# Causal attention with memory and two MoE blocks: scores of the last 64 queries for two pairs of heads at once, four rounds per couple of pairs

## The chip, the core and the metric

One core of a Trainium2 chip. The time is device microseconds (us) of one execution of the whole program, as the median of several runs. The engines of a core run side by side, each in its own order of instructions: PE (TensorE: matmuls and transposes), DVE (VectorE), ACT (ScalarE), POOL (GpSimd); SP only issues transfers. PEld is PE's loading of weights.

## The reference

```python
def _attn_ref(q, k, v, M_prev, z_prev, beta):          # B, H, S, D = 4, 8, 576, 64
    scores = scale * np.matmul(q, k.transpose(0, 1, 3, 2))
    causal = np.triu(np.ones((S, S), dtype=bool), k=1)
    scores = np.where(causal, -1000000000.0, scores)
    scores = scores - scores.max(-1, keepdims=True)
    a = np.exp(scores)
    a /= a.sum(-1, keepdims=True) + 1e-09
    local = np.matmul(a, v)
    ...
    mem_out = mem_ret / mem_norm                        # phi(q) @ M_prev, over phi(q) @ z_prev
    g = 1.0 / (1.0 + np.exp(-beta))[None, :, None, None]
    return g * mem_out + (1 - g) * local

def _moe_ref(x, w1, w2, w3, w_out):                     # 2304 tokens, 512 -> 1024 -> 512
    return ((x @ w1) * (x @ w2) @ w3) @ w_out

def _moe2_ref(x, w_in, w_out):                          # 512 -> 2048 -> 512
    h = x @ w_in
    return (h - np.tanh(h)) @ w_out
```

## The kernel before

The program has three stages: attention (to about 232 us), the first block of three products (to about 560), the second block (to the end). Only the attention is touched. Every instruction goes through one helper, so the profile gives all of them line 50; they are told apart by the names of their tiles.

**Attention.** The 32 heads (4 batches of 8) lie in 16 *pairs* `P`: head `h` of a pair has the 64 rows 64h to 64h+63 of the tile `r` (q and k, transposed, float32). The 576 queries of a head are five groups `u`: u = 0 to 3 with 128 queries, u = 4 with the last 64. A group needs keys 0 to 128(u+1) only, the last one all 576.

- `scores(m)`: a float32 matmul of 64 rows (the head's 64 dimensions) by 64 columns (64 queries) takes one quarter of PE's array. For u = 0 to 3 the two heads are the two row halves, the two halves of the 128 queries the two column halves (loop variable `y`), so that four matmuls use four quarters. For u = 4 there are only 64 queries: head h uses the quarter (rows h, columns h), two quarters at a time, and the 576 keys go in two parts of 288. Small bfloat16 matmuls (`maskb`) add the causal mask. Results lie in `sc`, a tile of two PSUM banks; there are two such tiles (`SB = 2`).
- `rmax(m)`: DVE takes the negated row maxima from `sc` into `st`. `exps(m)`: ACT writes exp(sc - max) to `p` and the sums to `st`; then that `sc` tile is free. `recip(m)` on DVE and `norm(m)` on POOL divide `p` by the sums, one round later.
- `trans(P, u)`: PE transposes `p` in blocks of 128 into `t` (two PSUM banks); ACT and DVE copy them to `g` (`g0` for u = 0, 1, `g1` for u = 2, 3 and the last group, `g2` for that group's last 64 keys). `av(P, grp)`: PE multiplies `g` by `v` into `o`, ACT copies that to `xs`. `av(P, 0)` is the queries of u = 0, 1 and `av(P, 1)` the rest.

**The order** of all engines within the attention is the order of the source (a helper chains each instruction to the one before it on its engine). A step `m` is one entry of `GROUPS = ((0, 1), (2,), (3,), (4,))`, so a pair has four steps, and the loop takes two steps at a time, a *round*: even rounds hold u = 0, 1 and u = 2, odd rounds u = 3 and u = 4. One round is, in this order: `recip` and `norm` of the two steps before; `scores` and `rmax` of both steps; `work(m)` (the exps of the first step and background jobs); one `av` of the pair before; `pieces` (see below); `trans` of the round before's first step; `work(m + 1)`; `pieces`; `trans` of its second step.

**Background.** `decode` jobs turn 30 loaded blocks of weights (`raw`, 512 KB each) into two float32r halves by operations on POOL (`T`, `E`, and the copy to `zs`, `fo`, `wa` or `wb`), ACT (`T`, `E`) and DVE; a new one begins at every step up to `LEAD`, then at every second. `fold_pe` multiplies w3 by w_out in pieces of three matmuls (`fo`), up to `PIECES[s]` of them at each of a pair's four steps. The memory part (`mw`, `mq`, `mt`, `mo`) runs as a job, too. After the last round the matmuls of the first block (`ab`) follow; PE may take them while it would wait in the last rounds.

**First loads.** SP's queue issues two parts of pair 0's `r`, three `raw`, then `r` of pair 1; ACT's queue issues the identity, the mask, the third part of pair 0's `r`, and `beta` (`gates`).

Of the kernel before, what the change touches and what calls it, by code (L numbers as in the profile page):

```python
# [33 lines left out]
def block_kernel(ctx, tc, qk, qt, vt, mp, zp_d, beta, w1, w2, w3t, wo, wi, wo2, ident_d, mask_d, out):  # L34
# [138 lines left out]
    def tp(o, i):  # L173
# [7 lines left out]
    PIECES = (1, 2, 0, 2)  # L181
    MEM, ROOM = 12, (1.5, 1.5, 1.75)
    LEAD, SHORT, TB, WX = 3, 9, 4, (0, 1, 2, 3, 4, 5)
# [9 lines left out]
        ("r", RB), ("1", 1), ("2", 2), ("4", 4), ("z", ZB), ("t", TB))]  # L193
# [58 lines left out]
    jobs, todo, raws, live = [], deque(fold_seq), [], [0]  # L252
# [7 lines left out]
    def decode(item):  # L260
# [4 lines left out]
        t = apt.tile([128, 512], U32, tag="T", name="T")  # L265
# [3 lines left out]
        e = ap2.tile([128, 512], U32, tag="E", name="E")  # L269
# [22 lines left out]
        DV.tensor_tensor(out=lo, in0=tf, in1=hi.bitcast(F32), op=ALU.subtract)  # L292
        if k[0] in range(8):
            folds.append((k, fstep[0]))
# [37 lines left out]
    if True:  # L332
# [6 lines left out]
        qk_cols(0, slice(320, 576), AC)  # L339
# [12 lines left out]
        first_q(320, 576)  # L352
# [38 lines left out]
        GROUPS = ((0, 1), (2,), (3,), (4,))  # L391
        NM = 16 * len(GROUPS)
# [3 lines left out]
        def step(m):  # L396
            P, s = divmod(m, len(GROUPS))
            return P, [(u, 128 * x) for x, u in enumerate(GROUPS[s])]

        def scores(m):  # L400
            P, us = step(m)
            q, k = qk_t[P][:, 0], qk_t[P][:, 1]
            hr = [(h, slice(64 * h, 64 * h + 64)) for h in range(2)]
            sc = sc_t[m] = pss.tile([128, 2, 512], F32, tag="sc", name="sc")
            qs = [(h, r, y, slice(64 * y, 64 * y + 64)) for y in range(2) for h, r in hr]
            for u, a in us:
                if u == 4:
                    continue
# [24 lines left out]
        def exps(m):  # L433
            P, us = step(m)
            st = st_t[m]
            for x, (u, a) in enumerate(us):
                sc = seen(m, u, a)
                p = p_t[P, u] = ap3.tile([128, PW[u]], F32, tag=f"p{u}", name="p")
                p = p[:].rearrange("p (a n) -> p a n", a=2)
# [34 lines left out]
        def trans(P, u):  # L474
            p = p_t.pop((P, u))
            if u == 0:
                g_t[0] = ap2.tile([128, 2, 2, 256], F32, tag="g0", name="g0")
            if u == 2:
                g_t[1] = ap1.tile([128, 4, 2, 320], F32, tag="g1", name="g1")
                g_t[2] = ap1.tile([64, 2, 64], F32, tag="g2", name="g2")  # L480
            if u < 4:
                K = 128 * u + 128
                blocks = [(kb, h) for kb in range(u + 1) for h in range(2)]
                for c in range(0, len(blocks), 4):
# [4 lines left out]
                    G = g_t[0] if u < 2 else g_t[1]  # L489
# [3 lines left out]
            else:  # L493
                t = psT.tile([128, 4, 128], F32, tag="t", name="t")
# [10 lines left out]
        def av(P, grp):  # L505
# [4 lines left out]
            hr = [(h, slice(64 * h, 64 * h + 64)) for h in range(2)]  # L510
# [4 lines left out]
            else:  # L515
                for kb in range(4):
                    q0 = 128 if kb == 3 else 0
                    for h, r in hr:
                        mm(o[r, q0:320], v[:, kb, h], g_t[1][:, kb, h, q0:320], kb == 0, False)
                for h, r in hr:  # L520
                    mm(o[r, 256:320], v[0:64, 4, h], g_t[2][:, h], False, True)
# [186 lines left out]
        coming, begun, active, owed = [0], [0], [0], [0]  # L708
        ahead()

        def background(m):
# [13 lines left out]
            if m >= coming[0] and begun[0] < len(fold_seq) and active[0] < TB:  # L725
# [15 lines left out]
        load_qk(1)  # L741
# [27 lines left out]

        m = 0  # L770
        while m < NM + 3 or jobs or late or folded[0] < 16 or begun[0] < len(fold_seq):
            P, s = divmod(m, 4)
# [6 lines left out]
            if m < NM:  # L779
                fill(FILL["s"].get(m, 0))  # L780
                for h in (m, m + 1):
                    scores(h)
                    rmax(h)
                if m == 0:
                    set_gates()
                if m == 2:
                    first_q(0, 576, 1)
            work(m)
            if 1 <= P <= 16:
                av(P - 1, s // 2)  # L790
                if s == 2 and P + 1 < 16:
                    load_v(P + 1)
            trs = 0 <= m - WAIT < NM
            flush_t()
            pieces(m, PIECES[s])
            if trs:
                fill(FILL["t"].get(m, 0))
                for u in GROUPS[(m - WAIT) % 4]:
                    trans((m - WAIT) // 4, u)
# [4 lines left out]
            if trs:  # L804
                for u in GROUPS[(m + 1 - WAIT) % 4]:
                    trans((m + 1 - WAIT) // 4, u)
# [383 lines left out]
```

## Time and profile before

| | |
|---|---|
| three runs | 968.78 us median (968.11 to 969.84) |
| the profiled execution | 971.45 us, its span 969.7 us |
| PE busy | 943.9 us, 97% of the span |
| DVE, ACT, POOL busy | 675.8, 623.1, 408.1 us (70, 64, 42%) |
| granted TensorE clock | 0.996 of full (2.4 GHz) on average |

The profiled execution took 971.45 us; its first to last instruction is the span, and 1.75 us lie around it. It is 2.67 us (0.28%) above the median of the runs. In the views, a row of the timeline or of the chain has its start and its duration; "x8" is the number of instructions merged into it (a float32 matmul of scores has two records); in square brackets stands idle time of the engine before the row and what ended it.

### The profile page before, as it was taken

What the parts mean: (1) busy time and instruction counts of PE and PEld (TensorE: products, weight loads), DVE (VectorE), ACT (ScalarE), POOL (GpSimd) and SP (SyncE); (2) the same over time, 40 slices, a digit from 0 to 9 for tenths busy, and PEclk for the clock granted to TensorE, in tenths of its full rate; (3) what the DMA queues carried; (4) which work ended last, traced back from release to release, by engine and by line L of the source; (5) the groups of instructions that cost most, each with busy time, mean ns of one, the idle gap of its engine ahead of it and who ended that gap; (6) DMA issues with size and microseconds to landing.
All of it is one profiled execution on the core that took longest, in us unless ns stands there. A gap on an engine that the chain in (4) does not pass through costs nothing.

```text
span 969.7 us, 16290 instructions
## 1 busy us (share of the span) xinstructions
PE 943.9 (97%) x5928; PEld 816.4 (84%) x5928; DVE 675.8 (70%) x1185; ACT 623.1 (64%) x1398; POOL 408.1 (42%) x500
## 2 busy tenths in 40 slices
PE   6899999999999999999999999999999999999998
PEld 3466666567989999999999999999999989999996
DVE  5778868897776743534424588887787887878875
ACT  5688887786546551323625587687777766776864
POOL 3768867786474521202406862222222222222222
PEclk9899999999999999999999999999999999999999
DMA  6455435422344530101401100000000000000000
GB/s 216 155 169 168 158 127 183 135 75 85 128 149 146 183 114 31 55 22 44 153 22 45 44 1 1 1 33 1 1 33 1 33 1 1 33 1 1 33 1 33
DMA packets 26080, 68.29 MB, mean 70 GB/s; under 512 B 4880, under 2 KB 5904, under 8 KB 26000
## 3 DMA queue, kind: packets, MB, share of 16 engines
q1 hardware_dynamic: 25296, 66.86, 20.8%
q8 instruction: 46, 0.75, 0.3%
q10 hardware_dynamic: 704, 0.40, 0.2%
q14 instruction: 34, 0.28, 0.1%
HBM read 62.53 MB, written 4.72 MB: 69 GB/s over the span
## 4 chain that ended last, share of the span: by engine, by line
PE 84%; DVE 7%; ACT 4%; POOL 2%; issue 1%; DMA 1%; ACTq 0%; DVEq 0%; POOLq 0%; SPq 0%
PE o L50 24%; PE h L50 21%; PE ab L50 19%; PE x L50 10%; PE sc L50 3%; PE t L50 3%; PE fo L50 3%; DVE st L50 2%; ACT p L50 2%; PE mo L50 2%; POOL p L50 1%; DMA r<-in_qk 1%; DVE g L50 1%; DVE mst L50 1%; DVE T L50 1%
## 5 line engine op out<-in xcount | busy, mean ns | idle before, releaser
L50 POOL TENSOR_TENSOR gl<-s,gh 128x384 fp32r<-128x384 f32 x96 | 99.7, 1038 | 288.0 <-ACT gh L50 274.9
L50 PE MATMUL x<-abh,wf 128*128 128x384 f32 x384 | 107.0, 342 | 1.1 <-ACT abh L50 1.1
L50 ACT ACTIVATE s<-u,pc 128x384 f32<-128x384 f32 x192 | 107.7, 613 | 0.6 <-POOL gl L50 0.6
L50 PE MATMUL ab<-xh,wa 128*128 128x384 f32 x384 | 106.9, 338 | 0.7 <-ACT xh L50 0.6
L50 POOL TENSOR_SCALAR p<-p,st 128x128 f32<-128x128 f32 (+2 forms) x144 | 86.1, 616 | 47.2 <-DVE st L50 41.0
L50 PE MATMUL ab<-xh,wb 128*128 128x384 f32 x384 | 105.9, 336 | 0.0
L50 DVE SCALAR_TENSOR_TENSOR s<-s,u 128x384 f32<-128x384 f32 x96 | 83.9, 874 | 26.8 <-ACT s L50 25.9
L50 ACT ACTIVATE p<-sc,st 128x128 f32<-128x128 f32 (+2 forms) x144 | 78.3, 556 | 29.7 <-DVE st L50 25.8
L50 ACT ACTIVATE u<-u,pc 128x384 f32<-128x384 f32 x96 | 59.4, 619 | 46.8 <-DVE s L50 46.8
L50 DVE TENSOR_TENSOR a<-ab,a 128x384 f32<-128x384 f32 x48 | 26.4, 552 | 77.4 <-PE ab L50 77.4
L50 PEld LDWEIGHTS x<-abh,wf 128*128 128x128 f32 x384 | 70.2, 188 | 5.6 <-issue 3.9
L50 POOL TENSOR_SCALAR E<-raw 128x512 f32<-128x512 f32 x72 | 53.9, 749 | 48.5 <-DVE z2p L50 13.1
L50 DVE TENSOR_TENSOR t<-h,t 128x384 f32<-128x384 f32 x96 | 53.1, 553 | 28.0 <-ACT t L50 27.5
L50 PEld LDWEIGHTS ab<-xh,wa 128*128 128x128 f32 x384 | 70.1, 188 | 2.0 <-ACT xh L50 0.9
L50 ACT ACTIVATE u<-h 128x384 f32<-128x384 f32 x96 | 46.7, 487 | 38.9 <-PE h L50 38.8
L50 PEld LDWEIGHTS ab<-xh,wb 128*128 128x128 f32 x384 | 70.1, 188 | 0.3 <-issue 0.3
L50 POOL TENSOR_SCALAR T<-raw 128x512 f32<-128x512 f32 x72 | 53.7, 746 | 39.2 <-DMA raw<-in_wo 12.0
L50 PE MATMUL sc<-r 64*64 64x128 f32 (+4 forms) x640 | 64.5, 457 | 5.8 <-DMA r<-in_qk 2.9
L50 DVE SCALAR_TENSOR_TENSOR s<-s,s 128x384 f32<-128x384 f32 x96 | 63.9, 665 | 8.7 <-DVE s L50 0.5
L50 PE MATMUL t<-ident,p 128*128 128x128 f32 (+1 forms) x400 | 58.2, 279 | 11.9 <-POOL p L50 4.4
L50 PEld LDWEIGHTS t<-ident,p 128*128 128x128 f32 (+1 forms) x400 | 45.2, 140 | 24.4 <-POOL p L50 6.4
L50 ACT ACTIVATE E<-raw 128x512 uint16<-128x512 uint32 x72 | 57.2, 795 | 12.6 <-POOL E L50 12.3
(208 smaller groups left out, 2538.3 us busy)
## 6 DMA issues: line engine op xcount, KB each, us to landing
raw<-in_wo SPq DMA_DIRECT2D x24, 512.0 KB, 3.5
r<-in_qk SPq DMA_DIRECT2D x15, 576.0 KB, 5.9
raw<-in_w3t SPq DMA_DIRECT2D x16, 512.0 KB, 4.0
raw<-in_w SPq DMA_DIRECT2D x16, 512.0 KB, 3.7
raw<-in_wi SPq DMA_DIRECT2D x16, 512.0 KB, 3.5
v<-in_vt SPq DMA_DIRECT2D x16, 320.0 KB, 2.9
mw<-in_qt SPq DMA_DIRECT2D x18, 256.0 KB, 3.5
out<-ob SPq DMA_DIRECT2D x18, 256.0 KB, 2.2
```

What stands on the lines that cost most here:

```text
L50: i = call(*args, **kw)
```

## The change

Two consecutive pairs, 2b and 2b + 1, now make a couple. `SEQ` gives the couple's eight steps, in four rounds:

| round | steps | `av` in it | transposes in it |
|---|---|---|---|
| s = 0 | first pair u = 0, 1; u = 2 | none | last groups of the couple before, the second head first |
| s = 2 | first pair u = 3; second pair u = 0, 1 | couple before, first pair, grp 1 | first pair u = 0, 1; u = 2 |
| s = 4 | second pair u = 2; u = 3 | couple before, second pair, grp 1; this couple, first pair, grp 0 | first pair u = 3; second pair u = 0, 1 |
| s = 6 | both last groups | second pair, grp 0 | second pair u = 2; u = 3 |

The last groups of both pairs are scored in one go, `scores_last`: one `sc` tile per head, rows of PE by head, columns by pair, so that four quarters work; both `sc` tiles are written from the start. The `p` of the second head's last groups takes the tile `p2`. The transposed last groups are copied in two halves, one per pair, one on ACT and one on DVE (twice: 128 partitions by 4x64, and 64 by 64). `g0` has one buffer in place of two, `g1` one for each pair of the couple. The buffers `T` and `E` of the decodes are now partly those that the later stages own, and a decode begins only when the fourth before it is done. `r` of two pairs is loaded in round s = 6 and scaled on ACT one and three rounds later. `r` of pair 0 comes in three parts through SP's queue, `r` of pair 1 right behind it and ahead of the `raw`; the scaling of the third part and of pair 1 moves behind the first maxima on DVE. `LEAD` is 2 in place of 3, and the loop runs one round longer at its end.

```diff
-    PIECES = (1, 2, 0, 2)
+    PIECES = (1, 2, 0, 2, 0, 2, 1, 2)
-    LEAD, SHORT, TB, WX = 3, 9, 4, (0, 1, 2, 3, 4, 5)
+    LEAD, SHORT, TB, WX = 2, 9, 4, (0, 1, 2, 3, 4, 5)
...
-        qk_cols(0, slice(320, 576), AC)
+        qk_cols(0, slice(320, 576))
...
-        first_q(320, 576)
...
-        GROUPS = ((0, 1), (2,), (3,), (4,))
-        NM = 16 * len(GROUPS)
+        SEQ = ((0, (0, 1)), (0, (2,)), (0, (3,)), (1, (0, 1)), (1, (2,)), (1, (3,)), (0, (4,)), (1, (4,)))
+        NM = 64
...
-            if us[0][0] == 4:
-                for x in range(2):
+
+        def scores_last(m):
+            P, us = step(m)
+            sc = [pss.tile([128, 2, 512], F32, tag="sc", name="sc") for _ in hr]
+            sc_t[m], sc_t[m + 1] = sc
+            for y in range(2):
+                for j, c in hr:
+                    q, k = qk_t[P + j][:, 0], qk_t[P + j][:, 1]
                     for h, r in hr:
-                        y = x ^ h
-                        mm(sc[r, y, 0:288], q[r, 512:576], k[r, 288 * y:288 * y + 288], True, y == 0)
+                        mm(sc[h][c, y, 0:288], q[r, 512:576], k[r, 288 * y:288 * y + 288], True, y == 0)
+            for j, c in hr:
                 for h, r in hr:
-                    mm(sc[r, 1, 224:288], identb[r, r], maskb[r, 0:64], False, True)
+                    mm(sc[h][c, 1, 224:288], identb[r, r], maskb[r, 0:64], False, True)
...
-                copy(g_t[1][:].rearrange("p a b q -> p (a b) q")[:, :, 256:320],
-                     t[:].rearrange("p a (b q) -> p (a b) q", b=2))
+                for j in range(2):
+                    copy(g_t[1, j][:, :, h, 256:320], t[:, :, 64 * j:64 * j + 64], on_act=j == 0)
                 t = psT.tile([128, 4, 128], F32, tag="t", name="t")
                 tp(t[0:64, 0], p[:, 512:576])
-                copy(g_t[2][:], t[0:64, 0].rearrange("p (b q) -> p b q", b=2), on_act=False)
+                for j in range(2):
+                    copy(g_t[1, j][0:64, 3, h, 0:64], t[0:64, 0, 64 * j:64 * j + 64], on_act=j == 0)
...
+        load_qk(1)
         ahead()
...
-            if m >= coming[0] and begun[0] < len(fold_seq) and active[0] < TB:
+            if m >= coming[0] and begun[0] < len(fold_seq) and active[0] < TB and turn[0] - 4 not in going:
...
-        load_qk(1)
...
+                if s == 6:
+                    scores_last(m)
                 for h in (m, m + 1):
-                    scores(h)
+                    if h == 1:
+                        first_q(320, 576)
+                    if h == 3:
+                        first_q(0, 576, 1)
+                    if s < 6:
+                        scores(h)
                     rmax(h)
...
-            if 1 <= P <= 16:
-                av(P - 1, s // 2)
...
+            if s == 2 and 1 <= b <= 8:
+                av(2 * b - 2, 1)
...
+            if s == 4 and 1 <= b <= 8:
+                av(2 * b - 1, 1)
...
+            if s in (4, 6) and b < 8:
+                av(2 * b + (s == 6), 0)
+            lots = (m - 2, m - 1) if s else (m - 1, m - 2)
...
-            if s == 0 and 1 <= P <= 16 - RB:
-                load_qk(P + RB - 1)
-            if s == 0 and 1 <= P < 15:
-                scale_q(P + 1)
+            if s == 6:
+                for P in (2 * b + 3, 2 * b + 4):
+                    if P < 16:
+                        load_qk(P)
+            if s == 0 and 1 <= b < 8:
+                scale_q(2 * b + 1)
+            if s == 4 and b < 7:
+                scale_q(2 * b + 2)
```

Two places show what stands where now. First PE, in the steady part of the attention: of a round that begins with u = 0, 1 and u = 2, what follows the scores, up to the next round's first scores. Before (`o` is `av`, `fo` the fold's pieces, `t` the transposes of the round before's two steps, u = 3 and then u = 4):

```order
L50 MATMUL o<-g_810,v_108 64x256 x2
L50 MATMUL o<-g_810,v_108 64x128 x2
L50 MATMUL fo<-wa_375,zs 128x512 x3
L50 MATMUL t<-ident,p 128x128 x8
L50 MATMUL fo<-wb_429,zs 128x512 x3
L50 MATMUL t<-ident,p 128x128 x4
L50 MATMUL t<-ident,p 64x128
L50 MATMUL sc<-r 64x512 x4
```

And now:

```order
L50 MATMUL fo<-wa_290,zs 128x512 x3
L50 MATMUL t<-ident,p 128x128 x4
L50 MATMUL t<-ident,p 64x128
L50 MATMUL fo<-wb_346,zs 128x512 x3
L50 MATMUL fo<-wa_377,zs 128x512 x3
L50 MATMUL t<-ident,p 128x128 x4
L50 MATMUL t<-ident,p 64x128
L50 MATMUL sc<-r 64x512 x4
```

The `av` has left this round, and the first transposes are those of a last group, whose `p` was the last thing that ACT wrote in the round before. In the rounds of steps 8, 48 and 56 the order has less `fo` there: none in the first two, one piece ahead of the transposes and none after in the third.

Second ACT, in the round that ends just ahead of the last groups' scores: from the exps of its first step to those of its second. Before (a round of u = 3 and u = 4; the exps of u = 4 free the second `sc` tile):

```order
L50 ACTIVATE p,st<-sc,st 128x512 x2
L50 ACTIVATE xs_354<-o,omgt 128x2x64
L50 ACTIVATE xs_445<-o,omgt 128x3x64
L50 ACTIVATE g_1004<-t 128x2x128
L50 ACTIVATE T<-T 128x512
L50 ACTIVATE p,st<-sc,st 128x576
```

And now, in round s = 4 (its second step is u = 3):

```order
L50 ACTIVATE p,st<-sc,st 128x384 x2
L50 ACTIVATE xs_607<-o,omgt 128x5x64
L50 ACTIVATE xs_1886<-o,omgt 128x4x64
L50 ACTIVATE g_1812<-t 128x4x128
L50 ACTIVATE E<-raw 128x512
L50 ACTIVATE p,st<-sc,st 128x512 x2
L50 ACTIVATE g_1912<-t 128x2x128
```

The exps that free the second `sc` tile now stand behind the copies of two `av` (5 and 4 times 64 columns) and of a whole chunk of transposes.

## Rows read from the trace of the kernel before

**Rows 1.** Stretches: us, busy time by engine, PEclk, DMA share, GB/s

```profile
25.00:35.00 10.00, 8.38 (x45) 4.26 (x47) 6.60 (x12) 6.23 (x15) 7.00 (x13) 0.66 0.46 165
...
64.88:147.50 82.62, 80.14 (x756) 52.58 (x760) 66.51 (x140) 69.48 (x188) 64.39 (x93) 1.00 0.47 158
147.50:232.00 84.50, 80.94 (x762) 52.74 (x763) 75.25 (x157) 64.64 (x177) 63.63 (x88) 1.00 0.38 130
...
300.00:560.00 260.00, 260.00 (x1539) 253.44 (x1538) 121.81 (x209) 113.69 (x228) 93.51 (x101) 1.00 0.24 76
```

**Rows 2.** The chain in two full rounds, 51.98 to 64.88 us: start, duration, what

```profile
51.98 1.60 PE sc L50 x26
53.58 0.81 PE o L50 x8
54.39 0.90 PE fo L50 x3
55.30 0.87 PE t L50 x8
56.17 0.70 PE fo L50 x3
56.87 0.71 PE t L50 x5
57.59 2.08 PE sc L50 x19
59.66 2.35 PE o L50 x20
62.02 0.81 PE t L50 x6
62.82 1.39 PE fo L50 x6
64.21 0.67 PE t L50 x6
```

**Rows 3.** Timeline of PE, 111.2 to 113.5 us: scores of u = 3 and u = 4

```profile
111.30 1.09 PE L50 MATMUL sc<-r 64*64 64x512 f32 x8
...
112.25 1.16 PE L50 MATMUL sc<-r 64*64 64x288 f32 x8
...
113.37 0.49 PE L50 MATMUL o<-g,v 128*64 128x320 f32 x2
```

**Rows 4.** Groups by form, 57 to 232 us: count, busy, mean ns, idle before

```profile
L50 POOL TENSOR_SCALAR p<-p,st 128x576 f32<-128x576 f32 x12 | 9.0, 747 | 0.0
...
L50 DVE COPY g<-t 128x512 f32<-128x512 f32 x25 | 17.2, 688 | 15.3 <-PE t L50 15.2
...
L50 DVE COPY g<-t 128x256 f32<-128x256 f32 x12 | 5.0, 419 | 3.6 <-PE t L50 3.5
...
L50 DVE COPY g<-t 64x128 f32<-64x128 f32 x13 | 3.6, 276 | 1.9 <-PE t L50 1.9
...
L50 ACT ACTIVATE g<-t 128x512 f32<-128x512 f32 x37 | 22.8, 616 | 6.6 <-PE t L50 6.5
L50 ACT ACTIVATE E<-raw 128x512 uint16<-128x512 uint32 x23 | 18.5, 804 | 0.0
L50 ACT ACTIVATE p<-sc,st 128x512 f32<-128x512 f32 x26 | 17.7, 693 | 7.7 <-DVE st L50 7.7
```

**Rows 5.** Timeline of all engines, 0 to 58 us: waits of the first rounds

```profile
10.76 1.87 PE L50 MATMUL sc<-r 64*64 64x384 f32 x8 [2.86 <-DMA r<-in_qk]
...
23.07 0.64 POOL L50 TENSOR_SCALAR T<-raw 128x512 f32<-128x512 f32 x1 [1.52 <-DMA raw<-in_wo]
...
25.40 0.33 PE L50 MATMUL t<-ident,p 128*128 128x128 f32 x1 [2.67 <-POOL p L50]
...
52.98 2.08 POOL L50 TENSOR_SCALAR p<-p,st 128x512 f32<-128x512 f32 x3 [2.73 <-DVE st L50]
```

**Rows 6.** Issues of transfers: queue, count, KB each, median us to landing

```profile
r<-in_qk SPq DMA_DIRECT2D x15, 576.0 KB, 5.9
```

More of the change, by code (lines that the diff above doesn't have):

```diff
@@ L251, in block_kernel @@
     folds, fstep, folded, fold_open = deque(), [0], [0], [False]
-    jobs, todo, raws, live = [], deque(fold_seq), [], [0]
+    jobs, todo, raws, live, turn, going = [], deque(fold_seq), [], [0], [0], set()
     def ahead():
@@ L264, in decode @@
         lw, hw = rb[:, :, 0], rb[:, :, 1].bitcast(F32)
-        t = apt.tile([128, 512], U32, tag="T", name="T")
+        n = turn[0]
+        turn[0] += 1
+        going.add(n)
+        t = (stg["T"] if n & 2 else apt).tile([128, 512], U32, tag="T", name="T")
         tf = t[:].bitcast(F32)
@@ L268, in decode @@
         yield 0, 0, 0.7
-        e = ap2.tile([128, 512], U32, tag="E", name="E")
+        e = (stg["E"] if n & 1 else ap1).tile([128, 512], U32, tag="E", name="E")
         PO.tensor_scalar(out=e[:].bitcast(F32), in0=hw, scalar1=2.0 ** -100, scalar2=2.0 ** -53,
@@ L396, in step @@
         def step(m):
-            P, s = divmod(m, len(GROUPS))
-            return P, [(u, 128 * x) for x, u in enumerate(GROUPS[s])]
+            b, s = divmod(m, 8)
+            j, us = SEQ[s]
+            return 2 * b + j, [(u, 128 * x) for x, u in enumerate(us)]
+        hr = [(h, slice(64 * h, 64 * h + 64)) for h in range(2)]
         def scores(m):
@@ L402, in scores @@
             q, k = qk_t[P][:, 0], qk_t[P][:, 1]
-            hr = [(h, slice(64 * h, 64 * h + 64)) for h in range(2)]
             sc = sc_t[m] = pss.tile([128, 2, 512], F32, tag="sc", name="sc")
@@ L437, in exps @@
                 sc = seen(m, u, a)
-                p = p_t[P, u] = ap3.tile([128, PW[u]], F32, tag=f"p{u}", name="p")
-                p = p[:].rearrange("p (a n) -> p a n", a=2)
+                p = p_t[P, u] = ap3.tile([128, PW[u]], F32, tag="p2" if u == 4 and P % 2 else f"p{u}", name="p")
+                p = p[:, 0:576 if u == 4 else PW[u]].rearrange("p (a n) -> p a n", a=2)
                 for h in [slice(0, 1), slice(1, 2)] if u < 4 else [slice(0, 2)]:
@@ L476, in trans @@
             if u == 0:
-                g_t[0] = ap2.tile([128, 2, 2, 256], F32, tag="g0", name="g0")
+                g_t[0] = ap1.tile([128, 2, 2, 256], F32, tag="g0", name="g0")
             if u == 2:
-                g_t[1] = ap1.tile([128, 4, 2, 320], F32, tag="g1", name="g1")
-                g_t[2] = ap1.tile([64, 2, 64], F32, tag="g2", name="g2")
+                g_t[1, P % 2] = ap1.tile([128, 4, 2, 320], F32, tag=f"g1{P % 2}", name="g1")
             if u < 4:
@@ L509, in av @@
             o = psA.tile([128, 512], F32, tag="o", name="o")
-            hr = [(h, slice(64 * h, 64 * h + 64)) for h in range(2)]
             if grp == 0:
@@ L768, in work, with lot @@
                 background(h)
+        def lot(h):
+            P, us = step(h)
+            for u, _ in us:
+                trans(P, u)
         m = 0
-        while m < NM + 3 or jobs or late or folded[0] < 16 or begun[0] < len(fold_seq):
-            P, s = divmod(m, 4)
+        while m < NM + 5 or jobs or late or folded[0] < 16 or begun[0] < len(fold_seq):
+            b, s = divmod(m, 8)
             fstep[0] = m
@@ L785, in block_kernel @@
                     set_gates()
-                if m == 2:
-                    first_q(0, 576, 1)
             work(m)
-            if 1 <= P <= 16:
-                av(P - 1, s // 2)
-                if s == 2 and P + 1 < 16:
-                    load_v(P + 1)
-            trs = 0 <= m - WAIT < NM
-            flush_t()
+            flush_t()
+            if s == 2 and 1 <= b <= 8:
+                av(2 * b - 2, 1)
+                if b < 8:
+                    load_v(2 * b)
+            if s == 4 and 1 <= b <= 8:
+                av(2 * b - 1, 1)
+                if b < 8:
+                    load_v(2 * b + 1)
+            if s in (4, 6) and b < 8:
+                av(2 * b + (s == 6), 0)
+            lots = (m - 2, m - 1) if s else (m - 1, m - 2)
+            trs = 0 < m <= NM
             pieces(m, PIECES[s])
@@ L797, in block_kernel @@
                 fill(FILL["t"].get(m, 0))
-                for u in GROUPS[(m - WAIT) % 4]:
-                    trans((m - WAIT) // 4, u)
+                lot(lots[0])
             work(m + 1)
@@ L804, in block_kernel @@
             if trs:
[L805 to L806 removed]
+                lot(lots[1])
             if sums and not fold_open[0]:
                 flush_o()
[L809 to L812 removed]
+            if s == 6:
[6 more added lines that the diff above has]
+                scale_q(2 * b + 2)
             if not todo and not raws and not wdec[0]:
```

12 lines of the change are left out of this document (6 added, 6 removed).

## The prediction, made before the changed kernel ran

> **What bounds the kernel now.** I read the busy time by stretches first [rows 1]. From 300 to 560 us PE is busy without a gap, so what the attention gains or loses ahead of that is passed on whole; the order behind the attention's last rounds is the same in both programs. In the attention PE has a gap of 2.5 us in 64.9 to 147.5 and of 3.6 us in 147.5 to 232: it is the bound, but not by far. In the first stretch ACT is busy 84% and DVE 80%, in the second DVE 89%. Then I read the chain through two full rounds [rows 2]: PE alone, 5.61 us (51.98 to 57.59) and 7.29 (to 64.88), 12.90 per pair and 25.8 per couple. So less PE work makes a round shorter only as long as what PE waits for in it (POOL's p, ACT's exps, copies by ACT and DVE) is ready earlier too, and none of them has much room. Before 58 us it is different: PE waits for loads and for POOL [rows 5], and from 25 to 35 us the granted clock was 0.66 of full, in part at the lower of the two levels (1.2 GHz), after the stretch in which PE stood 2.67 us.
>
> **Term 1, the scores of the last groups.** The timeline shows both kinds side by side [rows 3]. u = 3 runs on four quarters: 8 records, 4 matmuls of 512 columns, and from its start to that of the next scores 0.95 us (111.30 to 112.25), masks included. u = 4 on two quarters: also 8 records, of 288 columns only, and 1.12 us (112.25 to 113.37). At four quarters the 512 columns cost 0.95 us for 128 queries; at two, 2 x 288 = 576 columns in turn cost about as much for 64. `scores_last` puts 16 records into the same number of turns, two per quarter, so that a couple pays 1.12 us once where it paid it twice. The masks, four in place of twice two, go beside each other as those of u = 3 do. Eight couples: 8 x 1.12 = 9.0 us less of PE. Below: 0 if the quarters do not run side by side. Matmuls, transposes and `av` are otherwise the same in number.
>
> **Term 2, the transposes of the last groups come first in round s = 0.** From the chain's pieces [rows 2] the round's PE work is now scores 1.60, a piece 0.90, five transposes 0.71, two pieces 1.39, five transposes 0.71: 5.3 us, of which only 1.60 + 0.90 = 2.5 lie ahead of the first transposes, where 1.60 + 0.81 + 0.90 = 3.3 did. What they need: the last exps, then on DVE the copies of the previous transposes and two reciprocals, then on POOL the two `norm` of 0.75 us each [rows 4], the needed one second. In the round of rows 2 POOL began its norms 1.0 us after the first scores, after waiting for DVE [rows 5]; now DVE's copy ahead of it is of four blocks, not two, which is 0.27 us more (0.69 to 0.42) [rows 4]. So p is ready about 1.3 + 1.5 = 2.8 us into the round: a wait of 0.3 to 0.5 us where a piece stands ahead, and 1.2 in the rounds of steps 8 and 48, where none does. Step 56 has one piece ahead and none between, so it goes with the former. Five times 0.4 and twice 1.2: 4.4 us; I take 4.0, as DVE's copy is at times done sooner. Bounds 0 (ACT ends its last exps early, as the round s = 6 has the fewest) and 10 (1.2 or more in all seven).
>
> **Term 3, both score tiles at once.** `scores_last` needs both `sc` tiles free at the start of round s = 6; the second tile was wanted about 0.95 us into a round before. What frees it are the exps of u = 3 on ACT, which stand behind the copies of two `av`. On PE the round s = 4 is about 1.8 for the scores (u = 2 and u = 3; 0.95 the latter), 2.35 + 0.81 for the `av`, 0.87 for eight transposes, 1.39 for pieces, 0.67 for six [rows 2]: 7.9 us. On ACT: 1.8 + 3.16 + half of 0.87, then a chunk's copy of 0.62, E 0.80, and two exps of 0.69 [rows 4]: 8.2 us. Overlap of ACT's instructions takes some of that off, so 0.25 us of wait per couple: 2.0 us. Bounds 0 and 0.5 each (4.0).
>
> **Term 4, more copies.** A pair's last group cost DVE one copy of 0.28 us (64x128) and ACT one of 0.62. Now each has 128x256 and 64x64. On DVE that is 0.42 [rows 4] and about half to all of 0.28, so 0.35 more per pair; ACT loses about as much as it gains. Where DVE has room this is nothing; in 147.5 to 232 us, six pairs, it is 2.1 us on an engine that is busy 89% [rows 1]: I count half, 1.0 us, bounds 0 and 2.1.
>
> **Term 5, the start.** The third part of pair 0's `r` made PE wait 2.86 us and land at 10.76 [rows 5]. Now it follows the second part in one queue, ahead of the three `raw` and not beside them; I expect the scores of u = 2 at about 8 to 9. But half of it comes back: pair 1's u = 0, 1 are now scored in the second round, and their q is scaled on DVE behind the maxima of u = 3, while PE waits up to 2 us. The `raw` move behind another 576 KB; POOL's first `T` was not late by them. The fourth `raw` held POOL at 23.07, its norms behind it and PE for 2.67 us [rows 5]; with `LEAD` 2 that `T` stands behind the norms of two more steps, which covers it. Against it the first round with last groups has its waits for both tiles and for `g0`. Then the clock: 10 us at 0.66 cost 3.4 us [rows 1]; the new order has weak stretches there as well, so I count half of it. Together I take 3.0 us less, bounds 1 more and 6 less.
>
> **Costed at nothing.** `r` of the odd pairs is loaded one round ahead of its scaling, not two: the load needs only the scores of round s = 6 to be over and has then the rest of that round and most of the next, about 11 us, for a transfer of 5.9 us [rows 6]. If it were late, ACT would stand at the scaling with the exps of two steps behind it. One buffer of `g0`: the `av` that reads it stands ahead of the transposes that write it. Round s = 6 asks for `g0` after 1.1 us of scores, which cover a copy of 0.7. The rule that a decode begins only after the fourth before it is done shifts pieces to the end, five of them, where PE has the products of the first block beside them.
>
> **Sum.** -9.0 + 4.0 + 2.0 + 1.0 - 3.0 = -5.0 us on 971.45: 966.45 for such an execution. The runs' median is 2.67 below the profiled one, so 963.8 us.
>
> **The rivals.**
> - *All covers hold.* If terms 2 to 4 are nothing, as PE's gap of 6 us in 167 [rows 1] would have it, -12 us: 956.8.
> - *The evacuation becomes the bound.* ACT's and DVE's work per couple does not shrink, and a round's length is then their chain (maxima, exps, copies, reciprocals), not PE's sum. For it speaks DVE's 89%; against it that PE had two rounds without a gap [rows 2]. Term 1 is then waited away but for 1 us or so, and the start's 3 us half: about 966 to 969, no measurable change; 968. The Trainium skill, "TensorEngine Tiling (Array Packing)", Performance Considerations, "PSUM Bottleneck", says that tiling speeds up TensorE but not the emptying of PSUM, which may become the limit. By that rule the gain of term 1 would go, and the time is this rival's; the trace's 97% of PE against 80 to 89% of DVE bears it out only in the last third.
> - *Slower, by ACT in round s = 4.* Term 3 with the odd work that ACT has in some rounds (a partial sum's copy, the memory's exp, `mq`): three more instructions of about 0.6 us each [rows 4] put the exps 1.9 us behind PE in every couple, 15 us in all. With the other terms -9.0 + 4.0 + 15.2 + 1.0 - 3.0 = +8: 977; with six of the eight couples hit (11.4 us) it is 973, which I take. It decides where the wait passes 0.9 us per couple.
> - *The quarters do not run side by side.* In u = 3 the two matmuls of one row half read the same keys; now they read the tiles of two pairs. No row of before shows that. Then term 1 is 0, PE's longer scores cover term 3, and the time is 971.45 + 4.0 + 1.0 - 3.0, less 2.67: 970.8. Nothing in the trace speaks for it, since the matmuls are separate instructions there too.
>
> **How the numbers follow.** Chances: the forecast 0.46 (its own range 960 to 967), all covers 0.20, evacuation 0.14, slower by ACT 0.14, no quarters 0.06. A measurement of this kernel can tell about 0.2%, 1.9 us: faster is under 966.8, slower over 970.7. Faster: 0.43 of the forecast and 0.20 of the covers, with 0.02 of the evacuation: 0.65. Same: 0.03 of the forecast, 0.11 of the evacuation, 0.03 of the two last: 0.17. Slower: 0.18. The range goes from the full gain, 956.5, to where the slower cases begin, 971.
>
> **What would show it.** PE's `sc` of 64x288: 16 records within some 1.1 us, 8 couples, its total down by half. Waits "PE t <- POOL p" about 0.4 us in rounds s = 0, and "PE sc <- ACT p" about 0.25 us ahead of the last groups. DVE's busy share over 90% from 147 us on. The scores of u = 2 at 8 to 9 us, and no wait of POOL for a `raw` near 23 us. I am wrong if round s = 4 or s = 6 shows PE waiting over 1 us in most couples, or if PE's gaps in the steady part grow past 9 us.

## The result and the profile after

The changed kernel is slower by 0.9%: 977.82 us (median, 975.75 to 979.43) against 969.31 for the kernel before on the same chip, a ratio of 1.0088 with a 95% interval of [1.0063, 1.0114]. The forecast was 963.8, the range 956.5 to 971.0. Ratios below are always to the kernel before, measured in the same session.

Where the time went is read from three numbers per trace. The span less PE's busy time (first part of the page) is PE's idle time; half of PE's busy time in stretches with a granted clock of 0.50 (1.2 GHz) is lost to the clock; the rest is PE's work at full clock (2.4 GHz). The ends of matmuls are modelled in a trace: kernels with the same matmuls (before, e3, e9, e10) come to 938.2 to 941.8 in the last column, so it is good to some 3 us.

| kernel | span | PE busy | idle | lost to the clock | work at full clock |
|---|---|---|---|---|---|
| before | 969.7 | 943.9 | 25.8 | 3.1 | 940.8 |
| after | 977.7 | 943.8 | 33.9 | 9.4 | 934.4 |
| before with the new start alone (e3) | 961.0 | 942.1 | 18.9 | 1.6 | 940.5 |
| before with `LEAD` 2 alone (e9) | 959.2 | 938.2 | 21.0 | 0 | 938.2 |
| after with filling matmuls (e5) | 971.5 | 945.9 | 25.6 | 0 | 945.9, of it some 9 filling |

From before to after PE's work fell by 6.4 us, its idle time rose by 8.1 and the clock took 6.3 more: +8.0. Against e3, which has the new start and no couples, the work fell by 6.1, the idle time rose by 15.0 and the clock took 7.8 more: +16.7.

Stretches of the changed kernel, with the columns of [rows 1]; the last three are falls of the clock:

```profile
25.00:35.00 10.00, 6.19 (x68) 4.15 (x72) 9.11 (x17) 7.71 (x19) 8.94 (x11) 1.00 0.28 81
64.88:147.50 82.62, 78.44 (x752) 51.11 (x752) 63.76 (x147) 67.81 (x193) 67.74 (x94) 1.00 0.49 157
147.50:232.00 84.50, 76.23 (x699) 48.05 (x699) 65.25 (x144) 60.88 (x175) 55.90 (x83) 0.94 0.36 114
300.00:560.00 260.00, 259.39 (x1537) 252.46 (x1536) 120.83 (x211) 114.27 (x230) 90.59 (x100) 1.00 0.26 79
39.40:42.80 3.40, 3.10 (x17) 1.45 (x21) 1.99 (x9) 2.58 (x8) 0.52 (x2) 0.50 0.45 154
179.40:182.80 3.40, 3.01 (x17) 1.67 (x21) 1.50 (x6) 3.40 (x10) 1.22 (x2) 0.50 0.54 152
210.10:216.90 6.80, 6.30 (x47) 3.20 (x49) 5.78 (x15) 5.11 (x14) 5.74 (x10) 0.50 0.24 77
```

Against [rows 1] PE's gap grew from 2.5 to 4.2 us in the second row and from 3.6 to 8.3 in the third. DVE is busy 77% there where it was 89%: no engine became the bound, all stand more. The falls lie in or right behind the rounds of steps 8, 48 and 56, and the trace of e4 has the same three; two more are at 8.7 and 15.5 us, in the start. Those of the start come and go: with the same start, the traces of e4 and e5 have one and none there.

What PE waits for in the changed kernel: total us, times, longest; first 0 to 60 us,

```profile
PE t L50 <- POOL p L50: 4.2, 5, 1.5
PE sc L50 <- DVE r L50: 3.6, 3, 1.9
PE t L50 <- DVE g L50: 2.4, 2, 1.5
```

then 60 to 260 us:

```profile
PE t L50 <- POOL p L50: 5.0, 6, 1.5
PE t L50 <- DVE g L50: 2.9, 2, 1.5
PE o L50 <- ACT xs L50: 2.5, 4, 0.6
PE sc L50 <- ACT r L50: 1.7, 4, 0.9
...
PE sc L50 <- ACT p L50: 0.3, 1, 0.3
```

The wait for the normalised `p` was foreseen. The wait of transposes for DVE's `g`, up to 1.5 us, was not. The timeline of the round of step 48 (174.37 to 182.38 us; start, duration, what, and the idle time ahead of it; selected rows) shows how the two follow each other:

```profile
174.37 0.40 PE L50 MATMUL sc<-r 64*64 64x128 f32 x8
174.58 1.02 DVE L50 TENSOR_TENSOR xs<-mo,xs 128x384 f32<-128x384 f32 x2
175.11 0.85 PE L50 MATMUL sc<-r 64*64 64x384 f32 x8
176.03 1.89 DVE L50 TENSOR_REDUCE st<-sc 128x2 f32<-128x256 f32 x3
176.04 1.47 POOL L50 TENSOR_SCALAR p<-p,st 128x576 f32<-128x576 f32 x2 [2.49 <-DVE st L50]
177.15 0.37 ACT L50 ACTIVATE p<-sc,st 128x128 f32<-128x128 f32 x1 [2.17 <-DVE st L50]
177.56 0.77 PE L50 MATMUL t<-ident,p 128*128 128x128 f32 x5 [1.54 <-POOL p L50]
177.83 0.96 DVE L50 SCALAR_TENSOR_TENSOR T<-T,E 128x512 uint32<-128x512 uint32 x1
178.72 0.68 DVE L50 TENSOR_TENSOR wf<-s,wf 128x512 fp32r<-128x512 f32 x1
178.74 0.48 ACT L50 ACTIVATE g<-t 128x256 f32<-128x256 f32 x2
179.32 0.54 DVE L50 COPY g<-t 128x256 f32<-128x256 f32 x2
179.79 1.33 PE L50 MATMUL t<-ident,p 128*128 128x128 f32 x5 [1.46 <-DVE g L50]
181.04 1.56 PE L50 MATMUL mo<-mq,mc 64*64 64x384 f32 x8
182.38 1.23 PE L50 MATMUL sc<-r 64*64 64x512 f32 x8
```

No fold piece stands between. DVE reaches the reciprocals only behind two sums of `xs`, so POOL begins at 176.04 and both norms end at 177.5; PE's first five transposes start then and take both `t` buffers. ACT's half of their copy stands behind four exps (177.15 to 178.8), whose maxima DVE took behind the reciprocals. DVE's half stands behind those maxima and two background operations, `T` and `wf`: it starts at 179.32, as `wf` ends and 0.1 us after ACT's half, with no idle time ahead of it. At 179.79 PE has the buffers back. It stood 3.0 us, and from 179.4 it ran at 0.50. Step 56 is much the same (0.77, then 1.45, fall at 210.1). Step 8 has the same two waits (1.47, then 1.54, fall at 39.4), but there DVE did stand for ACT's half:

```profile
38.81 0.47 ACT L50 ACTIVATE g<-t 128x256 f32<-128x256 f32 x2
39.22 0.55 DVE L50 COPY g<-t 128x256 f32<-128x256 f32 x2 [1.27 <-ACT g L50]
```

The round of step 24 had one wait of 1.54 us, and no fall behind it.

The last groups themselves, PE at 138.74 us:

```profile
138.74 1.42 PE L50 MATMUL sc<-r 64*64 64x288 f32 x14
139.76 0.19 PE L50 MATMUL sc<-maskb,identb 64*64 64x64 bf16 x1
139.76 0.41 PE L50 MATMUL sc<-r 64*64 64x288 f32 x2
140.00 0.20 PE L50 MATMUL sc<-maskb,identb 64*64 64x64 bf16 x3
140.13 0.87 PE L50 MATMUL o<-g,v 128*64 128x256 f32 x8
```

Sixteen records to the next work take 1.39 us where twice 1.12 stood before [rows 3]: the quarters do work side by side. But they do not all start together. In the view that ends at 138.97 one record has begun; the other quarters start at 138.98, just behind the end of ACT's exps of u = 3 at 138.93. In the couple at 167.91, where those exps were done earlier, all start at once, and the next work follows after 1.16 us (first PE and ACT at 138.7 us, then PE at 167.91):

```profile
138.74 0.45 PE L50 MATMUL sc<-r 64*64 64x288 f32 x1
138.71 0.22 ACT L50 ACTIVATION_READ_ACCUMULATOR p<-sc,st 128x1 f32 x1
...
167.91 1.20 PE L50 MATMUL sc<-r 64*64 64x288 f32 x16
168.93 0.21 PE L50 MATMUL sc<-maskb,identb 64*64 64x64 bf16 x4
169.07 0.44 PE L50 MATMUL o<-g,v 128*64 128x256 f32 x2
```

The first record leads the others by 0.22 to 0.24 us in six of the eight couples; at 198.45 the others are 0.8 us late. PE is busy with what has started, so this does not show as idle time.

### The profile page after: what moved, and what is told of

The parts are those of the page before. It is cut to its first block, busy times and chain, and to the rows that moved or that the text cites. A ratio compares the mean times of both kernels' runs of the same rounds, so it can differ in the third digit from the quotient of the medians.

```text
span 977.7 us, 16299 instructions
## 1 busy us (share of the span) xinstructions
PE 943.8 (97%) x5927; PEld 814.0 (83%) x5928; DVE 674.4 (69%) x1201; ACT 622.2 (64%) x1414; POOL 414.4 (42%) x500
## 4 chain that ended last, share of the span: by engine, by line
PE 86%; DVE 6%; ACT 3%; POOL 2%; issue 1%; DMA 1%; SPq 0%; DVEq 0%; ACTq 0%; POOLq 0%
PE o L50 25%; PE h L50 21%; PE ab L50 19%; PE x L50 10%; PE sc L50 4%; PE t L50 3%; PE fo L50 3%; DVE st L50 2%; PE mo L50 2%; ACT p L50 2%; POOL p L50 1%; DVE g L50 1%; DVE T L50 1%; ACT E L50 1%; DMA r<-in_qk 0%
## 5 line engine op out<-in xcount | busy, mean ns | idle before, releaser
L50 POOL TENSOR_SCALAR p<-p,st 128x128 f32<-128x128 f32 (+3 forms) x144 | 94.1, 672 | 48.4 <-DVE st L50 38.4
L50 ACT ACTIVATE p<-sc,st 128x128 f32<-128x128 f32 (+3 forms) x144 | 77.6, 551 | 34.7 <-DVE st L50 34.1
L50 POOL TENSOR_SCALAR T<-raw 128x512 f32<-128x512 f32 x72 | 56.1, 779 | 40.5 <-DVE wa L50 10.2
L50 DVE COPY g<-t 128x256 f32<-128x256 f32 (+1 forms) x80 | 37.5, 485 | 42.9 <-PE t L50 32.9
L50 PE MATMUL sc<-r 64*64 64x128 f32 (+4 forms) x640 | 60.8, 467 | 6.4 <-DVE r L50 3.6
```

What stands on the lines that cost most here:

```text
L50: i = call(*args, **kw)
```

## The experiments

**Which part costs.** The new start alone on the kernel before (e3, its edit below), and the changed kernel with the old start (e7, the same edit undone):

```diff
-    LEAD, SHORT, TB, WX = 3, 9, 4, ...
+    LEAD, SHORT, TB, WX = 2, 9, 4, ...
...
-        qk_cols(0, slice(320, 576), AC)
+        qk_cols(0, slice(320, 576))
...
-        first_q(320, 576)
...
+        load_qk(1)
         ahead()
...
-        load_qk(1)
...
+                    if h == 1:
+                        first_q(320, 576)
```

> The kernel before with the new start alone: third part of pair 0's r through SP's queue, pair 1 right behind, the scaling of the third part behind the first maxima, LEAD 2. Theory: the start is not the loss; the scores of u = 2 begin at 8 to 9 us, not 10.8, and the stall of POOL near 23 us goes: 1 to 5 us faster than before, 964 to 968. Rival (the start is the loss, by the clock falls of 8.7 to 19 us): slower than before by 2 us or more, 971 or more.

> The changed kernel with the start of before (third part of r through ACT's queue, its scaling first, pair 1 behind the raw, LEAD 3). Theory (start and couples add): the start alone gave 6.6 us on the kernel before, so this is 5 to 7 us slower than the changed kernel, 982 to 985, and the couples alone cost 14 to 16. Rival (the couples' order needs pair 1 in the second round and gets nothing from the new start): 976 to 980.

Measured: e3 961.72 us, ratio 0.9927 [0.9903, 0.9951]; e7 988.41, ratio 1.0201 [1.0182, 1.022]. The start is worth 6.6 us on the kernel before and 10.6 on the changed one, so the couples, with their buffers and the rule for decodes, cost some 16 us (961.72 to 977.82) to 19 (before to e7). The loss is theirs, and the start hides about half of it.

**Which part of the start gains.** `LEAD` 2 alone (e9), and the loads alone (e10), on the kernel before:

> The kernel before with LEAD 2 in place of 3 and nothing else, so that the first products of the fold begin a step later. The new start as a whole took 6.6 us off the kernel before. Theory A: most of that is POOL's, because in the kernel before a fold's T waited for the fourth raw at 23.07 us, held the norms behind it and PE for 2.67 us, and the fall of the granted clock behind it (27.3 to 34.1 us) cost 3.1 us more; LEAD alone takes that away: 963 to 965 us. Theory B: most is the loads', PE's 2.86 us at 10.76 us and the order of the queue: LEAD alone moves the time by less than 1.5 us, 967 to 970 us.

> The kernel before with the new loads and no new LEAD: the third part of pair 0's r in the second part's queue, pair 1's r ahead of the raw tiles, and the scaling of the third part behind the first scores. Theory A (POOL's T is the cost): PE's wait at 10.76 us goes, about 2 to 3 us, and the wait behind the raw and the fall of the clock stay or come later: 965 to 968 us. Theory B (the loads are the cost): 962 to 963 us, as with the whole new start.

Measured: e9 962.55, ratio 0.9924 [0.9905, 0.9943]; e10 968.62, ratio 0.9982 [0.997, 0.9995]. `LEAD` alone gains as much as the whole start. In e10 PE waits 0.8 us for the third part of `r` in place of 2.9, but POOL still waits for a `raw` in front of the norms:

```profile
21.16 0.63 POOL L50 TENSOR_SCALAR T<-raw 128x512 f32<-128x512 f32 x1 [1.00 <-DMA raw<-in_wo]
21.89 2.93 POOL L50 TENSOR_SCALAR p<-p,st 128x512 f32<-128x512 f32 x3
...
23.47 0.33 PE L50 MATMUL t<-ident,p 128*128 128x128 f32 x1 [2.39 <-POOL p L50]
```

In e9 that `T` stands behind the norms and waits for nothing, and 25 to 35 us, at 0.66 in [rows 1], has the full clock in the profiled execution:

```profile
25.00:35.00 10.00, 8.40 (x92) 5.13 (x88) 8.70 (x18) 6.90 (x22) 8.48 (x14) 1.00 0.43 146
```

**Are the waits and the falls the loss?** Unread matmuls of 128 columns fill PE in the rounds of steps 8, 48 and 56, ahead of the first and of the second transposes (e1: 12 and 12, 12 and 12, 6 and 12; e5: 7 and 7, 7 and 7, 3 and 7):

```diff
             pieces(m, PIECES[s])
+            keep(m, 0)
...
                 pieces(m + 1, PIECES[s + 1])
+            keep(m, 1)
```

> The changed kernel with matmuls that nobody reads (12 of 128 columns, identity by identity, float32) ahead of the first and of the second transposes in the rounds of steps 8, 48 and 56 (6 ahead of the first in step 56). They fill waits and do no work. Theory (the waits of rounds s = 0 make the granted clock fall, and the fall costs as much as they): the falls near 39, 179 and 210 us go, in which PE was busy 3.1, 3.0 and 6.3 us at half speed, so 6 us less than the changed kernel, about 971 to 973, with PE's real waits as they were. Rival (the clock is a symptom, the rounds are as long whatever it does, since ACT and DVE set them): no change, 976 to 979.

> As the first filled kernel, with 7 matmuls in place of 12 (3 in place of 6): in that run 24 of them took about 3.9 us where the waits were 3.0, so that they made the rounds longer and paid back what the clock gave. Theory (a fall of the clock behind each long wait): rounds 8, 48 and 56 stay as long as in the changed kernel, the falls near 39, 179 and 210 us go, about 5 us faster than the changed kernel, 972 to 974. Rival (the falls are paid by waits anyway): 976 to 979.

Measured: e1 978.59, ratio 1.0097 [1.0072, 1.0122]; e5 973.3, ratio 1.004 [1.002, 1.006]. e1 tells nothing by its time, since its filling was longer than the waits (round 8 took 8.26 us, where it took 6.72; its 24 filling matmuls took 5.5 us, not 3.9 as the expectation for e5 has it). In e5 the clock does not fall once before the end of the span, and useless work makes the kernel 4.5 us faster: about half of the loss is the clock. The two falls of the start that its trace lacks are not the filling's doing; e16 below has the same filling, two falls in the start, none behind the three rounds, and the same time.

**The av moved into the round s = 0** (e2), and **the pieces of steps 46, 47, 54 and 55 held back** for rounds 48 and 56 (e6):

```diff
-            if s in (4, 6) and b < 8:
-                av(2 * b + (s == 6), 0)
+            if s == 4 and b < 8:
+                av(2 * b, 0)
+            if s == 0 and 1 <= b <= 8:
+                av(2 * b - 1, 0)
```

```diff
             owed[0] += n
+            if h in (46, 47, 54, 55):
+                return
```

> The changed kernel with the second pair's product for its first 256 queries moved from round s = 6 into the next round s = 0, ahead of the transposes. Theory (round s = 0 has too little on PE): 0.8 us more stands ahead of the first transposes, so that their wait falls from 1.5 to 0.7 us at steps 8, 24 and 48 and from 0.8 to 0 at step 56, 3 us, and one or two of the three clock falls go (1.5 to 3 us each): 972 to 975. Rival (PE waits for ACT and DVE over the whole couple, the place does not matter): the wait moves to round s = 6, 976 to 979.

> The changed kernel with the fold's pieces of steps 46, 47, 54 and 55 held back, so that rounds 48 and 56 have two pieces ahead of the first transposes and two between the batches. Theory (a round s = 0 without pieces is what stands, twice: for POOL's norm, and for the copies that free the two transpose tiles): PE's idle time in rounds 48 and 56 falls from 3.0 and 2.2 us to under 1 in sum, the clock falls behind them go (2.9 and 6.3 us at half speed), 6 to 8 us faster than the changed kernel, 970 to 972. Rival (ACT and DVE set the pace over the couple): the idle time turns up in rounds 46 and 54, 976 to 979.

Measured: e2 979.06, ratio 1.0111 [1.0076, 1.0147], no gain: PE's idle time in the round of step 48 went from 3.0 to 2.4 us only, as the second wait stayed (1.69). e6 975.58, ratio 1.0065 [1.005, 1.008]: rounds 48 and 56 lost their waits (3.0 and 2.2 us), but 1.0 came up in round 46, 0.9 in round 50 and 1.7 in round 54.

**Both halves copied by DVE** (e8; `on_act=j == 0` becomes `on_act=False` in `trans`), and **POOL's norms in the wanted order** (e13):

```diff
-                for h in (m - 2, m - 1):
+                for h in (m - 2, m - 1) if s else (m - 1, m - 2):
                     norm(h)
```

> The changed kernel with both halves of a last group's transposes copied by DVE (it waited for ACT's half of the same tile, which stands behind the exps of u = 0, 1). Theory (the second wait in rounds s = 0 is ACT's place in the line): the waits of 1.5 us between the two batches at steps 8, 48 and 56 fall to about half, 2 to 4 us faster with a clock fall less, 973 to 976; DVE has 0.6 us more per group. Rival (DVE is the bound from 147 us on): 978 or more.

> The changed kernel with POOL's two norms of a round s = 0 in the order in which the transposes want them: that of step m - 1 first. Theory: the first wait of that round (POOL's p, 9.2 us in 11 waits) is one norm of 0.75 us too long in each of seven rounds, of which about 0.5 us each comes back, as the reciprocals of both steps now stand ahead of it; with one fall of the clock less 972 to 975 us. Rival: the second wait, for the buffers of the transposes, takes its place, as it did when the av was moved: 976 to 979 us.

Measured: e8 975.33, ratio 1.006 [1.0043, 1.0076]. The time lies in the expected range by luck, for the second wait fell only in round 8 (1.54 to 0.83 us). In rounds 48 and 56 it grew, from 1.46 and 1.45 to 1.88 and 1.89, as the copies follow DVE's maxima, `T` and `wf` whoever takes the first half (e8, round 48):

```profile
172.47 0.96 DVE L50 SCALAR_TENSOR_TENSOR T<-T,E 128x512 uint32<-128x512 uint32 x1
173.35 0.68 DVE L50 TENSOR_TENSOR wf<-s,wf 128x512 fp32r<-128x512 f32 x1
173.96 1.00 DVE L50 COPY g<-t 128x256 f32<-128x256 f32 x4
174.85 0.74 PE L50 MATMUL t<-ident,p 128*128 128x128 f32 x5 [1.88 <-DVE g L50]
```

What e8 took away is elsewhere: PE's waits for ACT's scaling of `r` in four rounds (1.7 us in the changed kernel, none from 60 us on in e8), and DVE's waits. In the changed kernel DVE's copies of a shared tile waited 9.9 us for ACT's (0 to 260 us: count, busy, mean ns, idle before):

```profile
L50 DVE COPY g<-t 128x256 f32<-128x256 f32 x32 | 13.5, 421 | 13.6 <-ACT g L50 9.9 <-PE t L50 3.6
```

and in e8, with 16 copies more, not at all:

```profile
L50 DVE COPY g<-t 128x256 f32<-128x256 f32 x48 | 18.7, 417 | 7.5 <-PE t L50 7.2
```

e13: 976.96, ratio 1.0079 [1.0058, 1.01], not told from the changed kernel. The transposes' idle time is the same, only under other names, first in the changed kernel, then in e13:

```profile
L50 PE MATMUL t<-ident,p 128*128 128x128 f32 x384 | 56.8, 283 | 15.0 <-POOL p L50 9.2 <-DVE g L50 5.3 <-ACT g L50 0.3
```

```profile
L50 PE MATMUL t<-ident,p 128*128 128x128 f32 x384 | 55.4, 279 | 14.9 <-DVE g L50 6.3 <-POOL p L50 5.2 <-POOL wa L50 2.2
```

So the rival held in the sum: waits for DVE's `g` and for POOL's `wa` took the place of the first one.

**Do the shorter scores pay?** The last groups' matmuls issued twice (e14), and their order changed so that one pair's come first (e4):

```diff
+            for n in range(2):
...
-                        mm(sc[h][c, y, 0:288], ..., True, y == 0)
+                            mm(sc[h][c, y, 0:288], ..., True, n == 0 or y == 0)
```

> The changed kernel with the sixteen records of 64x288 of a couple issued twice (the first pass is written over by the second), so that PE's scores of the last groups are about 1.0 us longer in each of eight couples. Theory A: PE is the bound in the round s = 6, the shorter scores pay there, and doubling costs most of 8 us: 983 to 986 us. Theory B (the evacuation is the bound): the round's end is set by ACT, DVE and POOL behind the scores or the longer scores are made up in the waits of the round s = 0: under 980 us, and the idle of PE in the rounds s = 0 grows less or shrinks.

> The changed kernel with the last groups' matmuls in the order pair, keys, head: the two pairs one after the other, so that only two quarters work most of the time and three turns of 0.48 us are needed where two were. Theory (the four quarters do save PE time): 0.4 to 0.5 us more per couple, 3 to 4 us slower than the changed kernel, 980 to 982. Rival (PE's time at this place is hidden by waits anyway): 976 to 979, no change.

Measured: e14 983.25, ratio 1.014 [1.0116, 1.0163], 5.4 us over the changed kernel; e4 977.39, ratio 1.0082. The busy time of that form is 11.7 us in the changed kernel, 18.6 in e9 and 19.4 doubled:

```profile
L50 PE MATMUL sc<-r 64*64 64x288 f32 x128 | 11.7, 415 | 0.1
```

```profile
L50 PE MATMUL sc<-r 64*64 64x288 f32 x128 | 18.6, 408 | 0.0
```

```profile
L50 PE MATMUL sc<-r 64*64 64x288 f32 x256 | 19.4, 409 | 0.1
```

Of 7.7 us more on PE 5.4 reach the end, and that although e14's trace lost 4.7 us less to the clock, 3.2 of it in the start that it does not touch: PE is still the bound there, and the saving of term 1 was real. e4 failed as an experiment: its trace has the rows of the changed kernel, 1.41 us to the next work at 138.09 us where it was 1.39, whichever pair is issued first, so it took nothing away.

**The new buffers and the rule for decodes** (e11: on top of e3) and **a second piece at the couple's start** (e15: `PIECES` 2, 2, 0, 2, 0, 2, 0, 2):

> The kernel before with the new start, and on top the new buffers of T and E (two shared with the staging pool) and the rule that a decode begins only after the fourth before it. If these cost nothing, as predicted, it stays at 961 to 963 us, that of the new start alone. Rival: the rule starts pieces later and the shared buffers make POOL wait; then some of the 16 us by which the couples are slower than the new start alone is theirs, and it comes out at 965 us or more.

> The changed kernel with the second table's 1 and 1 put together at the couple's start (PIECES 2, 2, 0, 2, 0, 2, 0, 2): a second piece of 0.7 us ahead of the first transposes of the round s = 0, taken from the round s = 6. Theory: the first wait is covered in rounds that have pieces (16, 24, 32, 40), about 0.5 us each, none in 8, 48 and 56, where no piece is to be had: 975 to 977 us. Rival: the round s = 6 needs its piece as much, and waits for POOL and ACT in its place: 978 to 980 us.

Measured: e11 964.72, ratio 0.9942 [0.9924, 0.9961]; e15 977.06, ratio 1.0084 [1.0061, 1.0107]. e11 is 3.0 us over e3 as it stands and 1.5 by the ratios, whose intervals overlap: a small cost, not settled. Its trace has 168 of the fold's 192 matmuls ahead of the attention's last transposes, as the changed kernel has; e3 has 177, before 183. So 9 of the 15 that the changed kernel lacks as cover go with the buffers and the rule, and 6 with the start, whose kernels are the fastest here. e15 moved waits and saved none.

**The repairs together.** e12: held pieces, DVE copies, filling in rounds 8 and 56, and the head order of the last scores reversed (`for h, r in hr[::-1]`). e16: the norms' order, e15's pieces, the reversed heads and e5's filling:

> The changed kernel with four repairs together: DVE copies both halves of the last groups, the pieces of steps 46, 47, 54 and 55 are held back for rounds 48 and 56, filling matmuls of 128 columns stand in the uncovered round of step 8 (7 and 7) and 56 (3 and 7), and the head order of the last scores is reversed so that the matmul that waits for ACT comes first. If the repairs add (2.5 and 2.2 us as measured alone, about 2 of the 4.5 us of the filling, and one turn of 0.24 us in six couples): about 970 us, level with the kernel before and 8 above the new start alone. Rival: they take away the same waits and the same falls of the clock, so that the largest decides: 972 to 974 us. If the couples had a gain of 5 us or more that waits alone hide, it would come under 965 us.

> The changed kernel with the norms in the wanted order, the pieces as in e15_pc, the head order of the last scores reversed and the filling of 7 matmuls in rounds 8, 48 and 56. If single waits are the cause and add up: 968 to 971 us. If the chain of the round s = 0 (exps, reciprocals, norms, transposes, copies) sets its length whatever PE does in it: 972 to 976 us, no better than the filling alone (973.3).

Measured: e12 976.17, ratio 1.0066 [1.0047, 1.0085]; e16 973.14, ratio 1.0038 [1.0025, 1.0052]. They don't add: e12 is no better than either of its first two parts alone, e16 no better than the filling alone. The reversal did not line the quarters up. In e16 the first record still leads, by 0.22 to 0.24 us in four couples and 0.13 in three, and the next work starts 1.38 us behind it where it was 1.39 (e16; the first row from a view that ends at 137.70):

```profile
137.49 0.45 PE L50 MATMUL sc<-r 64*64 64x288 f32 x1
...
138.87 0.87 PE L50 MATMUL o<-g,v 128*64 128x256 f32 x8
```

No version of the couples reached the kernel before. Those that beat it are all without couples, e3 (961.72) and e9 (962.55) first.

## Why the prediction was wrong, step by step

- **Term 1** (-9.0): the mechanism is right, and nearly the size. Where all four quarters start at once, start to next work is 1.16 us: 2 x 1.12 - 1.16 = 1.08 us per couple, 8.6 in eight. In most couples it is 1.39, because term 3's wait stands in it; so the form's busy time fell by 6.9 only.
- **Term 2** (+4.0) is the step that failed. It counted one wait, for POOL, and stopped there: it did not ask what the next five transposes need. In seven rounds PE stood 3.01, 0.57, 1.54, 0.41, 0.17, 3.00 and 2.22 us (steps 8 to 56): 10.9 in all, past the upper bound of 10. Three rounds with a piece ahead came out near the forecast's 0.4; in step 24 POOL did an `E` just ahead of the norms. In the two longest (8 and 48) the foreseen 1.2 was 1.5, and a second wait of 1.5 followed, for the two `t` buffers that ACT and DVE empty behind their own exps, maxima and background work. That step 56 "goes with the former" was wrong as well: 2.2 us.
- **Term 3** (+2.0): mechanism and size were right, though the wait is no idle time of PE. The other quarters were 0.22 to 0.24 us late in six couples, 0.8 in one and not at all in one, 2.2 us in all. Beside it the two `av` of a round s = 4 collided, which no term had: four of these rounds waited 0.63 us each for ACT's copy of the first, as the second follows at once: 2.5 us. The rival that put 12 us and more in this round fell, though its time came close; that was luck.
- **Term 4** (+1.0) priced the copies by DVE's busy share, and DVE was not short of time (77%). What cost was their place: in rounds 48 and 56 behind DVE's own maxima and background work, in round 8 behind ACT.
- **Term 5** (-3.0): right in that the start gains, wrong in why. The loads are worth 1.1 us (e10), `LEAD` 7.1 (e9): in the kernel before a `T` ahead of the norms waited 1.52 us [rows 5], PE then 2.67, and behind that came the fall of [rows 1].
- **The clock** was counted for the start only. Three rounds of the steady part got falls of their own (39.4, 179.4 and 210.1), which half of 3.10, 3.01 and 6.30 us of busy time puts at 6.2 us. The prediction had the row for it, PE's 2.67 us and the 0.66 behind [rows 1, 5], and did not carry it to the rounds in which it forecast waits.
- **Costed at nothing**: `r` of the odd pairs did make PE wait, 1.7 us in four rounds, not by its load but by the place of its scaling on ACT. The fold has 15 matmuls less ahead of the attention's end (183 to 168), which are the five pieces that were named; what was not priced is that they are missing as cover in the rounds.
- **The evacuation as the bound** was nearer than its chance, though not in the prediction's form. The Trainium skill's rule there ("TensorEngine Tiling (Array Packing)", Performance Considerations, "PSUM Bottleneck"), that the emptying of PSUM may become the limit of tiled matmuls, shows in the 2.2 us at the last groups' scores; but in the round s = 6 e14 shows PE still setting the time. The second waits of rounds 8, 48 and 56, 4.5 us, are waits for emptying too, but of transposes, which take the whole array (128*128).

As an estimate, the terms with what was measured give -8.6 + 10.9 + 4.7 + 1.7 + 6.2 - 6.6 (scores, rounds s = 0, term 3 with the `av`, `r`, clock, start by e3) = +8.3 us, where +8.5 was measured. That it fits so well is in part chance, as waits that the kernel before had in the same places are not taken off.

Of its own signs "PE's gaps past 9 us" came true (12.5 in the two rows against 6.0), and the scores of u = 2 at 8 to 9 us (8.6). Waits over 1 us in s = 4 or s = 6 did not, nor DVE over 90%.

What stays open: why the repairs do not add. The likeliest reading, argued and not shown, is that exps, reciprocals, norms, transposes and copies of a round s = 0 form one chain, with a length of its own, so that freeing one link leaves the next. The link that the rows of rounds 48 and 56 point at, DVE's copies put ahead of its `T` and `wf`, was not tried.

## What to carry to other kernels

When a step is moved to a place with less work ahead, follow it to the end of its chain: not only to what it waits for, but to who empties its buffers and what that engine does first. Price the waits of a round on PE twice, as idle time and as a fall of the clock behind it: here the three rounds with 2.2 to 3.0 us of waits were each followed by one. Look for waits also where an engine is busy: here the late quarters did not show as idle time. And take a change apart: a single constant held all of the gain, and the part that the change was named for held the loss.

## What was not expected of the hardware

- With the two pairs issued one after the other (e4), the matmuls of a last group took as long as with the two in turn: 1.41 us and 1.39 to the next work. The order of issue did not decide how many quarters worked.
- Unread work made a kernel faster (e5, 4.5 us), as it kept the granted clock at 1.00 behind the three rounds.
- A quarter of PE can work while the others wait: the first record of a last group ran 0.24 us ahead of the rest (138.74 and 138.98 us).
